# First slab on centred tokens: gate and up products scaled by ScalarE on the way out, its normalized tokens turned by one DMA, and the first y tiles seeded

## The chip, the cores and the metric

The kernel runs on one core of one Trainium2 chip. The metric is the device time of that core in microseconds (us), the median of repeated runs. One execution is recorded by the hardware profiler; all times inside the kernel below are counted from the start of that recorded span.

The core has a matrix engine (TensorE, "PE" in the profile), a vector engine (VectorE, "DVE"), an engine for functions of one operand (ScalarE, "ACT"), a general engine (GpSimd, "POOL"), and a queue engine (SyncE, "SP") that here issues nearly all DMA transfers. Each engine works through its own list of instructions in order and waits for semaphores of the others. "PEld" is the loading of a matmul's stationary operand, which runs beside PE.

## What is computed

For 2048 tokens `x` of width 512:

```python
xn = layernorm(x)                          # (x - mean) / sqrt(var + 1e-5), per token
# branch A: a complex diagonal recurrence of 512 states over time
Lam_bar = exp(dt * (Lambda_re + 1j * Lambda_im));  dt = exp(log_dt)
B_bar   = ((Lam_bar - 1) / Lam)[:, None] * (B_re + 1j * B_im)
Bu = einsum("bld,pd->blp", xn, B_bar)
h[t] = Lam_bar * h[t-1] + Bu[t]
s = 2 * einsum("blp,dp->bld", h, C_re + 1j * C_im).real + xn * Dskip
# branch B: a gated feed-forward layer of inner width 1376, then silu
g = silu((gelu(xn @ w_gate) * (xn @ w_up)) @ w_down)
out = x + s * g
```

The matrices and tokens are bf16.

## The kernel before

The tokens are worked in four slabs of 512 (`NS = 4`, `TS = 512`), a slab in four tiles of 128 tokens (`M = 4`). A tile's m below is 0 to 3. Tokens lie on the partitions when they are normalized, but a matmul needs the feature dimension there, so every normalized tile has to be turned (transposed): into `xnT`. Slab 0's tiles are turned by TensorE itself (a matmul with the identity into a spare PSUM bank, then a copy out of PSUM); the tiles of the later slabs are turned by a DMA (`dma_start_transpose`).

The instruction order on each engine isn't written down. The code collects steps with costs, and a planner in the kernel (`Plan`) sorts them by list scheduling and a random search; the text below therefore speaks of the order as built. TensorE's steps keep the order of the code.

Slab 0's gate and up products run in three chunks of columns, `CH0 = [(0, 384), (384, 896), (896, 1376)]`, each as pairs (gate in one PSUM bank, up in another) in one of three two-bank slots, one pair in the two spare banks `ybank`:

```python
def norm_dve(s, m):                      # VectorE, one pass: (x - mean) * rstd
    dve(512, lambda: V.tensor_scalar(out=xn[m][:], in0=x_tok[:, s * M + m, :],
        scalar1=mv[:, s, m, 0:1], scalar2=rs[:, s, m : m + 1],
        op0=ALU.subtract, op1=ALU.mult), ...)

def head_t(m):                           # turned by TensorE, copied out by ACT (m = 3: by DVE)
    transposed(xn[m], m, xnT[:, :, m * P : (m + 1) * P], [("xn", m)], [("xnT", 0, m)],
               m % 2, DVE if m == 3 else ACT)

def gate_pair(s, m, c, then=((), ()), spare=False):
    ...
    for bank, (nm, wt) in enumerate((("wg", wg), ("wu", wu))):
        def f(bank=bank, wt=wt):
            for k in range(KT):          # KT = 4
                T.matmul(pss[bank][:, 0:w], lhsT=xnT[:, k, t0 : t0 + P], rhs=wt[:, k, a:b], ...)
    acts(w, lambda: act(out=ud, in_=pss[1][:, 0:w], func=AF.Copy), both, [("ub", q)])
    acts(w, lambda: act(out=gd, in_=pss[0][:, 0:w], func=AF.Gelu_apprx_tanh), both, [("gt", q)], table="gelu", ...)
    dve(w, lambda: V.tensor_tensor(out=at[j][:, a:b], in0=gd, in1=ud, op=ALU.mult), ...)
```

`mv` holds mean and variance of a tile (from two VectorE instructions, L402 and L406), and `rs` its 1/sqrt(var + eps), a power computed by GpSimd (L409). The head of the program in the order of the code:

```python
dummies(6, 0); columns(); dummies(3, 0)           # dummy matmuls keep TensorE busy
stats(0, 0); mean(0, 0); rstd(0, 0, 1)
stats(0, 1); mean(0, 1); norm_dve(0, 0); rstd(0, 1, 2)
head_t(0); dummies(2, 0, 3); turn_angles(); angle(0)
norm_dve(0, 1); stats(0, 2); mean(0, 2); rstd(0, 2, 3); ...
stats(0, 3); norm_dve(0, 2); mean(0, 3); rstd(0, 3, 4); ...; norm_dve(0, 3)
tables()                                          # sine tables, on ACT and DVE
then = {0: ((lambda: head_t(1), spread), ()), 1: ((lambda: head_t(2),), ()), 2: ((lambda: head_t(3),), ())}
for m in range(M):
    gate_pair(0, m, 0, then.get(m, ((), ())), m == M - 1)
...
for m in range(M): gate_pair(0, m, 1)
for h in range(2): half(0, h)                     # B_bar products of slab 0, then the recurrence
for m in range(M): gate_pair(0, m, 2); at_t(0, m, 0, 2)
```

`half(s, h)` multiplies `BT` (the turned B matrices) with a slab's `xnT` on TensorE (L612), rotates the result by the tables, runs the scans and rotates back on VectorE, and leaves the states in `hst`. `at_t` turns the gated activations of a tile by DMA into `atT` (L527). `down_pair` multiplies `atT` with `wd` (L544), two tiles in one slot. Once slab 0's products are issued, slab 1 follows: `norm1` computes statistics and normalizes on VectorE, `dma_t` turns each tile (L453), `half(1, 0)` and `half(1, 1)` follow on TensorE, then `down_pair(0, 0)` (tiles 0 and 1) and `down_pair(0, 1)` (tiles 2 and 3). `norm_act(s)` does the normalization of slabs 2 and 3, with ScalarE for the sums and the scaling.

`y_tile` gives the output of branch A for a tile: eight matmuls of 512 columns (L574) into `ybank`, to which the skip term `sk = xn * Dskip` is added. From the third tile on ScalarE writes `sk` into the bank first ("seed") and the matmuls add to it; the first two tiles have no seed:

```python
if seed:
    acts(w, lambda: act(out=bank, in_=sk[s % 2][:, m, a:z], func=AF.Copy), ...)
...
if seed:
    dve(w, lambda: V.tensor_tensor(out=yg[e][:, a:z], in0=bank, in1=g2[gi][:, b, a:z], op=ALU.mult), ...)
else:
    dve(512, lambda: V.tensor_tensor(out=ys, in0=bank, in1=sk[s % 2][:, m, :], op=ALU.add), ...)
    dve(512, lambda: V.tensor_tensor(out=yg[e][:], in0=ys, in1=g2[gi][:, b, :], op=ALU.mult), ...)
```

All large transfers are issued by SyncE on one queue. As built, before: the four tiles of x of slab 0 mixed with the first weight chunks, second weight chunks, x of slab 1, `BT` (two DMA transposes of 512x512), third weight chunks, `wd`, four DMA transposes for slab 1's `xnT`, the two of C (into the memory of `hst[1]`), x of slabs 2 and 3, then the four `atT` of slab 0 in the order m = 0, 1, 3, 2.

Of the kernel before, what the change touches and what calls it, by code (L numbers as in the profile page):

```python
# [202 lines left out]
def kernel(  # L203
# [17 lines left out]
    nc = tc.nc  # L221
# [32 lines left out]
    xnT = sb("xnT", [P, KT, 2 * TS])  # L254
# [20 lines left out]
    xn = [sb(f"xn{i}", [P, D]) for i in range(M)]  # L275
# [5 lines left out]
    tF = sb("tF", [P, 2, D], FP32)  # L281
    junk = sb("junk", [P, D])
# [31 lines left out]
    def dma_first(eng, issue, land, emit, writes, **kw):  # L314

        first[eng] = dma(eng, issue, land, emit, writes=writes, after=[first[eng]] if eng in first else (), **kw)
# [29 lines left out]
    dma_first(SP, 1.45, 4.0, lambda: nc.sync.dma_start(out=x_tok[:, M : 2 * M, :], in_=x_r[:, M : 2 * M, :]), [("x", 1, m) for m in range(M)])  # L346
    for ri, src in enumerate((A_B_re, A_B_im)):
        dma_first(SP, 2.4, 4.0, lambda ri=ri, src=src: nc.sync.dma_start_transpose(out=BT[:, ri, :, :], in_=src), [("BT", ri)])
    for which in range(2):
        load_w(dma_first, SP, nc.sync, 2, (1.35, 4.1), which)  # L350
# [21 lines left out]
    def columns():  # L372

        pe(1, 150, lambda: T.matmul(rows, lhsT=pv[0][:], rhs=ident[0 : 2 * NPT, 0 : 2 * NPT], start=True, stop=True),
            [("pv", 0), ("pv", 1), "ident"], [("slot", 2, 0)])
        acts(4, lambda: act(out=dt_, in_=rows[:, 0:NPT], func=AF.Exp), [("slot", 2, 0), "tiny"], ["dt"], table="exp", rank=150.0)
        acts(1, lambda: act(out=tiny[:], in_=zero[:], func=AF.Sin), ["zero", "dt"], ["tiny"], table="silu", rank=150.0)
# [44 lines left out]
    def transposed(src, n, dst, reads, writes, bank, evict):  # L422
        tp = ybank[bank][:].bitcast(BF16)[:, 0:D].rearrange("p (k t) -> p k t", t=P)

        def f():
            for k in range(KT):
                T.transpose(tp[:, k, :], src[:, k * P : (k + 1) * P], ident[:])  # L427
        pe(KT, P, f, reads + ["ident"], [("y", bank)])
        if evict == ACT:
            acts(512, lambda: act(out=dst, in_=tp, func=AF.Copy), [("y", bank)], writes, rank=100.0)  # L430
        else:
            dve(512, lambda: V.tensor_copy(out=dst, in_=tp), [("y", bank)], writes, rate=2.0, rank=40.0)
# [10 lines left out]
    def norm_dve(s, m):  # L443
        dve(512, lambda: V.tensor_scalar(  # L444
            out=xn[m][:], in0=x_tok[:, s * M + m, :], scalar1=mv[:, s, m, 0:1], scalar2=rs[:, s, m : m + 1],
            op0=ALU.subtract, op1=ALU.mult), [("x", s, m), ("mv", s, m), ("rs", s, m)], [("xn", m)], rate=2.0)

# [3 lines left out]
    def dma_t(s, m):  # L451
        c0 = (s % 2) * TS + m * P
        return dma(SP, 1.2, 4.5 if s == 1 else 1.3, lambda: nc.sync.dma_start_transpose(out=xnT[:, :, c0 : c0 + P], in_=xn[m][:]),  # L453
            [("xn", m)], turned_tile(s, m))

    def skip(s, m):
        dve(512, lambda: V.tensor_tensor(out=sk[s % 2][:, m, :], in0=xn[m][:], in1=Drow[:], op=ALU.mult),
            [("xn", m), "Drow"], [("sk", s % 2, m)], rate=2.0)
# [4 lines left out]
    def gate_pair(s, m, c, then=((), ()), spare=False):  # L463

        if spare:
            pss, both = [ybank[0][:], ybank[1][:]], [("y", 0), ("y", 1)]
        else:
            i, ps = slot()
            pss, both = [ps[:, 0, :], ps[:, 1, :]], [("slot", i, 0), ("slot", i, 1)]
        a, b = CH0[c]  # L470
        w = b - a
        j = (s * M + m) % NAT
        t0 = (s % 2) * TS + m * P
        q = gu_n[0] % (2 * NGT)
        gu_n[0] += 1
        qb, qo = q // 2, (q % 2) * 512
        for bank, (nm, wt) in enumerate((("wg", wg), ("wu", wu))):
            def f(bank=bank, wt=wt):
                for k in range(KT):
                    T.matmul(pss[bank][:, 0:w], lhsT=xnT[:, k, t0 : t0 + P], rhs=wt[:, k, a:b], start=(k == 0), stop=(k == KT - 1))  # L480
            pe(KT, w, f, turned_tile(s, m) + [(nm, c)], [both[bank]])
            for t in then[bank]:
                t()
        gd, ud = gt[qb][:, qo : qo + w], ub[qb][:, qo : qo + w]
        acts(w, lambda: act(out=ud, in_=pss[1][:, 0:w], func=AF.Copy), both, [("ub", q)])
        acts(w, lambda: act(out=gd, in_=pss[0][:, 0:w], func=AF.Gelu_apprx_tanh), both, [("gt", q)], table="gelu", after=early if c == 0 else (), rank=40.0 if c + m == 0 else 0.0)
        dve(w, lambda: V.tensor_tensor(out=at[j][:, a:b], in0=gd, in1=ud, op=ALU.mult), [("gt", q), ("ub", q)], [("at", j, c)], rate=2.0)

    def gate_tile(s, m):

        j = (s * M + m) % NAT
        t0 = (s % 2) * TS + m * P
# [3 lines left out]
        def mm(ps, bank, wt, c):  # L496
            a, b = CH[c]

            def f():
                for k in range(KT):  # L500
                    T.matmul(ps[:, bank, 0 : b - a], lhsT=xnT[:, k, t0 : t0 + P], rhs=wt[:, k, a:b], start=(k == 0), stop=(k == KT - 1))  # L501
            return f
# [50 lines left out]
    def y_tile(s, m):  # L553
        i = y_n[0] % 2
        seed = y_n[0] >= 2
# [7 lines left out]
        for bank, key, a, z in parts:  # L563
            y_part(s, m, bank, key, a, z, i, e, gi, b, seed)

    def y_part(s, m, bank, key, a, z, i, e, gi, b, seed):

        w = z - a
        if seed:
            acts(w, lambda: act(out=bank, in_=sk[s % 2][:, m, a:z], func=AF.Copy), [("sk", s % 2, m)], [key])  # L570

        def f():
            for j in range(2 * NPT):
                T.matmul(bank, lhsT=hst[s % 2][:, j // NPT, j % NPT, m * P : (m + 1) * P], rhs=C2[:, j // NPT, j % NPT, a:z],  # L574
                         start=(j == 0 and not seed), stop=(j == 2 * NPT - 1), skip_group_check=True)
        pe(2 * NPT, w, f, [("hst", s % 2, 0), ("hst", s % 2, 1)] + C2S + ([key] if seed else []), [key])
        if seed:
            dve(w, lambda: V.tensor_tensor(out=yg[e][:, a:z], in0=bank, in1=g2[gi][:, b, a:z], op=ALU.mult),  # L578
                [key, ("g2", gi)], [("yg", e, a)], base=0.13)
        else:  # L580
            ys = tF[:, i, :]
            dve(512, lambda: V.tensor_tensor(out=ys, in0=bank, in1=sk[s % 2][:, m, :], op=ALU.add),
                [key, ("sk", s % 2, m)], [("tF",)], base=0.13)
            dve(512, lambda: V.tensor_tensor(out=yg[e][:], in0=ys, in1=g2[gi][:, b, :], op=ALU.mult),
                [("tF",), ("g2", gi)], [("yg", e, a)], base=0.13)
# [16 lines left out]
    def half(s, h):  # L602
# [3 lines left out]
        for q in range(H2):  # L606
            i, ps = slot()
            pt = h * H2 + q
            for ri in range(2):
                def f(ri=ri, pt=pt, ps=ps):  # L610
                    for k in range(KT):
                        T.matmul(ps[:, ri, :], lhsT=BT[:, ri, k, pt * P : (pt + 1) * P], rhs=xnT[:, k, (s % 2) * TS : (s % 2 + 1) * TS],  # L612
# [99 lines left out]
    def head_t(m):  # L712
        transposed(xn[m], m, xnT[:, :, m * P : (m + 1) * P], [("xn", m)], [("xnT", 0, m)], m % 2, DVE if m == 3 else ACT)

    def spread():
        pe(1, 512, lambda: T.matmul(slots[2][:, 1, :], lhsT=warm[0:1, 0:P], rhs=Drow[0:1, :], start=True, stop=True), ["Drow", "warm"], [("slot", 2, 1)])
        acts(512, lambda: act(out=Drow[:], in_=slots[2][:, 1, :], func=AF.Copy), [("slot", 2, 0), ("slot", 2, 1)], ["Drow"])
# [3 lines left out]
    dummies(3, 0)  # L721
# [3 lines left out]
    rstd(0, 0, 1)  # L725
    stats(0, 1)
    mean(0, 1)
    norm_dve(0, 0)
    rstd(0, 1, 2)
    head_t(0)  # L730
    dummies(2, 0, 3)
    turn_angles()
    angle(0)
    norm_dve(0, 1)
    stats(0, 2)
    mean(0, 2)
    rstd(0, 2, 3)
    angle(1)
    stats(0, 3)
    norm_dve(0, 2)  # L740
    mean(0, 3)
    rstd(0, 3, 4)
    angle(2)
    angle(3)
    norm_dve(0, 3)
    pl.in_turn = False
    tables()
    then = {0: ((lambda: head_t(1), spread), ()), 1: ((lambda: head_t(2),), ()), 2: ((lambda: head_t(3),), ())}
    for m in range(M):
        gate_pair(0, m, 0, then.get(m, ((), ())), m == M - 1)  # L750
        if m == 1:
            damping()
    dma_first(SP, 3.6, 4.3, lambda: nc.sync.dma_start(out=wd[:, 0 : NFT - 1, :], in_=B_w_down[0 : (NFT - 1) * P, :].rearrange("(k p) d -> p k d", p=P)), ["wd"])
    dma_first(SP, 0.4, 4.3, lambda: nc.sync.dma_start(out=wd[:FL, NFT - 1, :], in_=B_w_down[(NFT - 1) * P : F, :]), ["wd"])
    for m in range(M):
        skip(0, m)
    for m in range(M):
        gate_pair(0, m, 1)
    for h in range(2):
        half(0, h)  # L760
    for m in range(M):
        gate_pair(0, m, 2)
# [40 lines left out]
    def norm_out(s, m):  # L803
        acts(512, lambda: act(out=xn[m][:], in_=x_tok[:, s * M + m, :], func=AF.Identity, scale=rs[:, s, m : m + 1], bias=nb[:, s, m : m + 1]),
# [35 lines left out]
    for ri, src in enumerate((A_C_re, A_C_im)):  # L840
        dma(SP, 2.4, 5.0, lambda ri=ri, src=src: nc.sync.dma_start_transpose(out=CT[:, ri, :, :], in_=src),
            writes=[("CT", ri)], after=[turned[1]])
# [68 lines left out]
```

## Time and profile before

| what | value |
|---|---|
| time, median of 3 runs | 181.27 us (180.87 to 182.46) |
| recorded span | 179.6 us, granted TensorE clock 0.998 |
| TensorE busy | 173.4 us (97%) |
| VectorE busy | 157.8 us (88%) |
| ScalarE busy | 116.7 us (65%) |
| DMA queue of SyncE | 17.86 MB, 46.3% of 16 engines' span |
| first product of slab 0 on TensorE | at 6.21 us |
| second chunk's first product | at 13.41 us |
| first down product | at 40.61 us |

Read the busy shares first, then where the busiest engine is idle, and only then what the other engines do in those places. In the strip of 40 slices a slice is 4.49 us, and a digit is the busy share in tenths. Times in a timeline are the start of a merged run of instructions from its first to its last. A line such as "SPq" is the issue of a transfer, not the transfer: how long the data took is told apart, as the time from issue to landing.

### The profile page before, as it was taken

Reading aid. Unit: us, or ns where it says so; the run is one execution under the profiler, and the core shown is the slowest. Engines: PE = TensorE matmul, PEld = TensorE weight load, DVE = VectorE, ACT = ScalarE, POOL = GpSimd, SP = SyncE. Lnnn points to the kernel's source line nnn. Section 1 sums busy time; section 2 is a strip of 40 time slices with the busy share of each in tenths; the row PEclk is TensorE's granted clock in tenths of the full one; section 3 lists DMA queues with packets and bytes.
Section 4 is the critical chain, followed back from the end, with each engine's and each line's share of the span. In section 5 each row is a group of like instructions: output and inputs, shape, how many; then the busy total and the mean of one; then the engine's idle time right before and its main releaser. Section 6 shows DMA issues by size and latency. Waiting matters only on the chain.

```text
span 179.6 us, 2392 instructions
## 1 busy us (share of the span) xinstructions
PE 173.4 (97%) x838; PEld 82.6 (46%) x854; DVE 157.8 (88%) x268; ACT 116.7 (65%) x178; POOL 9.7 (5%) x19
## 2 busy tenths in 40 slices
PE   7999999999999999999999999999999999999992
PEld 2354444444445555444445554544445555444451
DVE  4789999998999999999999999999999999950063
ACT  4788599589999999645359964426618666353220
POOL 3230230000002000000020000000000000000000
PEclk9999999999999999999999999999999999999999
DMA  4999999997000429630011485050100084420011
GB/s 127 332 285 218 367 202 179 305 156 155 0 0 0 80 57 114 130 61 0 0 60 62 93 155 109 1 111 4 58 29 0 2 160 84 82 86 29 0 58 58
DMA packets 47109, 18.01 MB, mean 100 GB/s; under 512 B 38425, under 2 KB 47098, under 8 KB 47098
## 3 DMA queue, kind: packets, MB, share of 16 engines
q1 hardware_dynamic: 47072, 17.86, 46.3%
q8 instruction: 6, 0.10, 0.2%
q14 instruction: 5, 0.04, 0.1%
q10 hardware_dynamic: 26, 0.00, 0.0%
HBM read 6.33 MB, written 2.10 MB: 47 GB/s over the span
## 4 chain that ended last, share of the span: by engine, by line
PE 90%; DMA 4%; DVE 2%; SPq 1%; issue 1%; DVEq 0%
PE slot L501 31%; PE slot L544 21%; PE slot L612 15%; PE ybank L574 13%; PE slot L480 9%; DMA x_tok<-in_A_x_dram 3%; DMA out_dram<-ot 1%; DVE ot L586 1%; PE ybank L480 1%; SPq L328 1%; DVE yg L578 1%; SPq L321 1%; DVE st L402 0%; PE ybank L427 0%; DVE xn L444 0%
## 5 line engine op out<-in xcount | busy, mean ns | idle before, releaser
L501 PEld LDWEIGHTS <-xnT 128*128 128x128 bf16 x288 | 28.2, 98 | 28.4
L544 PE MATMUL slot<-wd,atT 128*128 128x512 bf16 (+1 forms) x173 | 38.5, 379 | 0.2
L501 PE MATMUL slot<-wu,xnT 128*128 128x512 bf16 (+1 forms) x144 | 31.8, 357 | 0.0
L501 PE MATMUL slot<-wg,xnT 128*128 128x512 bf16 (+1 forms) x139 | 31.5, 356 | 0.3
L645 DVE TENSOR_TENSOR_SCAN Fs<-rho,ini,W 128x512 bf16<-128x512 f32 x24 | 29.4, 1269 | 0.0
L612 PE MATMUL slot<-xnT,BT 128*128 128x512 bf16 x124 | 28.1, 379 | 0.2
L574 PE MATMUL ybank<-C,hst 128*128 128x512 bf16 (+1 forms) x125 | 27.6, 372 | 0.2
L544 PEld LDWEIGHTS <-atT 128*128 128x128 bf16 (+1 forms) x176 | 17.2, 98 | 20.9
L615 ACT ACTIVATE U<-slot 128x1024 bf16<-128x1024 f32 x16 | 16.0, 1021 | 12.5 <-PE slot L612 12.5
L578 DVE TENSOR_TENSOR yg<-ybank,g 128x512 bf16<-128x512 f32 (+1 forms) x14 | 9.4, 670 | 12.8 <-PE ybank L574 12.5
L574 PEld LDWEIGHTS <-hst 128*128 128x128 bf16 x136 | 13.3, 98 | 13.8
L612 PEld LDWEIGHTS <-BT 128*128 128x128 bf16 x128 | 12.5, 98 | 15.1
L626 DVE TENSOR_TENSOR Q<-U,tab 128x4096 bf16<-128x4096 bf16 x8 | 18.3, 2289 | 0.2
L626 DVE TENSOR_TENSOR Q<-Fs,tab 128x4096 bf16<-128x4096 bf16 x8 | 18.3, 2289 | 0.1
L548 ACT ACTIVATE g<-slot 128x1024 f32<-128x1024 f32 x8 | 8.2, 1021 | 13.4 <-PE slot L544 13.4
L570 ACT ACTIVATE ybank<-sk 128x512 f32<-128x512 bf16 (+1 forms) x14 | 8.1, 586 | 12.7 <-DVE yg L578 12.0
L509 ACT ACTIVATE gt<-slot 128x1024 bf16<-128x1024 f32 x12 | 12.3, 1023 | 3.7 <-PE slot L501 3.7
L509 ACT ACTIVATE ub<-slot 128x1024 bf16<-128x1024 f32 x12 | 12.2, 1020 | 3.0 <-PE slot L501 2.8
L480 PEld LDWEIGHTS <-xnT 128*128 128x128 bf16 x96 | 9.0, 98 | 9.7 <-ACT xnT L430 0.7
L823 ACT ACTIVATE junk<-x_tok 128x512 bf16<-128x512 bf16 x16 | 10.0, 627 | 1.6 <-DMA x_tok<-in_A_x_dram 1.4
L480 PE MATMUL slot<-wg,xnT 128*128 128x480 bf16 (+2 forms) x43 | 10.4, 360 | 0.4 <-ACT xnT L430 0.4
L480 PE MATMUL slot<-wu,xnT 128*128 128x512 bf16 (+2 forms) x44 | 10.4, 360 | 0.0
(118 smaller groups left out, 179.1 us busy)
## 6 DMA issues: line engine op xcount, KB each, us to landing
out_dram<-ot SPq DMA_DIRECT2D x15, 128.0 KB, 1.7
x_tok<-in_A_x_dram SPq DMA_DIRECT2D x3, 512.0 KB, 5.8
wd<-in_B_w_down_dram SPq DMA_DIRECT2D x1, 1280.0 KB, 9.9
x_tok<-in_A_x_dram SPq DMA_DIRECT2D x4, 128.0 KB, 3.0
wg<-in_B_w_gate_dram SPq DMA_DIRECT2D x1, 512.0 KB
wu<-in_B_w_up_dram SPq DMA_DIRECT2D x1, 512.0 KB, 6.9
wg<-in_B_w_gate_dram SPq DMA_DIRECT2D x1, 480.0 KB, 5.0
wu<-in_B_w_up_dram SPq DMA_DIRECT2D x1, 480.0 KB
```

Source lines behind the costliest of these rows:

```text
L480: T.matmul(pss[bank][:, 0:w], lhsT=xnT[:, k, t0 : t0 + P], rhs=wt[:, k, a:b], start=(k == 0), stop=(k == KT - 1))
L501: T.matmul(ps[:, bank, 0 : b - a], lhsT=xnT[:, k, t0 : t0 + P], rhs=wt[:, k, a:b], start=(k == 0), stop=(k == KT - 1))
L509: acts(1024, lambda ps=ps, dst=dst, fn=fn: act(out=dst[:, 0:1024].rearrange("p (c w) -> p c w", c=2), in_=ps[:, :, :], func=fn), [("slot", ...
L544: T.matmul(ps[:, b, :], lhsT=atT[:fs, k, m * P : (m + 1) * P], rhs=wd[:fs, k, :], start=(k == 0), stop=(k == NFT - 1))
L548: acts(1024, lambda: act(out=g2[gi][:, :, :], in_=ps[:, :, :], func=AF.Silu), [("slot", i, 0), ("slot", i, 1)], [("g2", gi)], table="silu" ...
L574: T.matmul(bank, lhsT=hst[s % 2][:, j // NPT, j % NPT, m * P : (m + 1) * P], rhs=C2[:, j // NPT, j % NPT, a:z], start=(j == 0 and not seed ...
L578: dve(w, lambda: V.tensor_tensor(out=yg[e][:, a:z], in0=bank, in1=g2[gi][:, b, a:z], op=ALU.mult), [key, ("g2", gi)], [("yg", e, a)], base ...
L612: T.matmul(ps[:, ri, :], lhsT=BT[:, ri, k, pt * P : (pt + 1) * P], rhs=xnT[:, k, (s % 2) * TS : (s % 2 + 1) * TS], start=(k == 0), stop=(k ...
L615: acts(1024, lambda q=q, ps=ps: act(out=U[ui][:, :, q, :], in_=ps[:, :, :], func=AF.Copy), [("slot", i, 0), ("slot", i, 1)], [("U", ui, q)])
L626: dve(4096, lambda: V.tensor_tensor(out=Qf, in0=src.unsqueeze(1).to_broadcast(WQ), in1=table, op=ALU.mult), reads, ["Q"], rate=2.0)
L645: pl.add(DVE, 1.116 if s == 0 else 1.19, lambda ri=ri, q=q, pt=pt, first=first: V.tensor_tensor_scan(out=Fs[:, ri, q, :], data0=rho[:, pt ...
L823: acts(512, lambda i=i, fn=fn, m=m: act(out=junk[:], in_=x_tok[:, s * M + m, :], func=fn, accum_out=sx[:, s, i, m : m + 1]), [("x", s, m)] ...
```

## The change

Three things are altered in slab 0 and in the first y tiles, and with them the order of the transfers.

1. For the first two chunks (c = 0 and 1) the gate and up products no longer take normalized tokens but tokens less their mean. A row's 1/sqrt(var + eps) is one number per token, so it can be applied to the row of the product: ScalarE applies it as it copies the product out of PSUM (`scale=rs[...]`, one number per partition, for the copy of up and before the gelu of gate alike). The turning by TensorE then waits for the mean alone and not for GpSimd's power.
2. The normalized tokens of slab 0 are still needed: for the B products, for chunk 2 and for the skip term. They are computed later, and turned all four tiles at once by one DMA.
3. The first two y tiles are seeded as the others are.

The centred tokens use memory that is free then (`Fs`, and `W` for the turned ones). The transfers are re-ordered: x of slab 1 is no longer loaded ahead of `BT`, C comes ahead of slab 1's turning, and `wd` behind it. The diff, cut to its core:

```diff
-    xnT = sb("xnT", [P, KT, 2 * TS])
+    xnT = [sb(f"xnT{i}", [P, KT, TS]) for i in range(2)]
+    xc = [Fs[:, i // 2, i % 2, :] for i in range(M)]
+    xcT = W[:].rearrange("p r q t -> p (r q t)").rearrange("p (m k t) -> p m k t", m=M, k=KT)
...
-    dma_first(SP, 1.45, 4.0, lambda: nc.sync.dma_start(out=x_tok[:, M : 2 * M, :], ...)
-    for ri, src in enumerate((A_B_re, A_B_im)):  ... BT ...
-    for which in range(2):
-        load_w(dma_first, SP, nc.sync, 2, (1.35, 4.1), which)
+    def load_rest():
+        ... BT, re and im ...
+        dma_first(SP, 2.0, 3.5, lambda: nc.sync.dma_start_transpose(
+            out=xnT[0]... , in_=xn_all[:].rearrange("p m d -> p (m d)")), ...)
+        ... x of slab 1, third chunk of wg and wu, C re and im ...
...
+    def center(m):
+        dve(512, lambda: V.tensor_scalar(out=xc[m], in0=x_tok[:, m, :], scalar1=mv[:, 0, m, 0:1],
+            scalar2=None, op0=ALU.subtract), [("x", 0, m), ("mv", 0, m)], [("xc", m)], rate=2.0)
...
+            kw, rd, ptr = {}, [], 0
+            if self.bare:                      # chunks 0 and 1
+                kw, rd, ptr = dict(scale=rs[:, 0, m : m + 1]), [("rs", 0, m)], 1
+            acts(w, lambda: act(out=ud, in_=pss[1][:, 0:w], func=AF.Copy, **kw), ...)
+            acts(w, lambda: act(out=gd, in_=pss[0][:, 0:w], func=AF.Gelu_apprx_tanh, **kw), ...)
...
-    dummies(3, 0)
+    dummies(1, 0)
     stats(0, 0); mean(0, 0)
-    rstd(0, 0, 1)
+    center(0)
     stats(0, 1); mean(0, 1)
-    norm_dve(0, 0); rstd(0, 1, 2); head_t(0); dummies(2, 0, 3)
+    center(1); rstd(0, 0, 2)
     ...
+    head_t(0, ACT); dummies(2, 0); behind = [head_t(1, ACT)]
+    ... # sine table of ACT asked for only now
+    pairs = [GatePair(m, 0, m == M - 1) for m in range(M)]
+    pairs[0].products(0); spread(); pairs[1].products(0); pairs[0].products(1)
+    head_t(2, ACT); pairs[1].products(1); damping(); pairs[2].products(0)
+    head_t(3, DVE); norm_dve(0, 1); norm_dve(0, 2); norm_dve(0, 3)
+    pairs[2].products(1); pairs[3].products(0); pairs[3].products(1)
...
     norm1()
-    for ri, src in enumerate((A_C_re, A_C_im)): ... C ...
+    first[SP] = turned[1]
+    ... wd, in two transfers ...
```

In `y_part` the branch without a seed is removed. The last pair of chunk 1 goes to the spare banks, so that the slots of the pairs behind it move by one; the sequence of products on TensorE is otherwise as before from chunk 0's end on.

## The prediction

> **What bounds the kernel now.** I read the busy shares first, then the waits of TensorE, then the chain of waits, then the timeline of the first 50 us.
>
> ```profile
> PE 173.4 (97%) x838; PEld 82.6 (46%) x854; DVE 157.8 (88%) x268; ACT 116.7 (65%) x178; POOL 9.7 (5%) x19
> ...
> DMA  4999999997000429630011485050100084420011
> ```
>
> TensorE is busy 97% of the span. The DMA strip has nines until about 45 us: the transfers are full exactly where the change re-orders them. The waits of TensorE up to 60 us:
>
> ```profile
> PE slot L419 <- DVE zero L362: 1.1, 1, 1.1
> PE ybank L427 <- DVE xn L444: 0.4, 1, 0.4
> PE slot L480 <- ACT xnT L430: 0.4, 1, 0.4
> ```
>
> All three lie before 10 us; from 14 us to the end the same view is empty. From the chain of waits (start, duration, what):
>
> ```profile
> 3.23 5.05 DMA x_tok<-in_A_x_dram
> ...
> 8.30 0.69 DVE st L402
> ...
> 9.36 0.40 PE ybank L427 x4
> ...
> 12.23 1.34 PE ybank L480 x8
> 13.58 0.21 PE slot L480
> 13.84 6.64 PE slot L480 x30
> ```
>
> x of tile 3 lands at 8.28, and VectorE finishes its statistics ahead of normalizing tile 2, so tile 2 is turned only at 9.36. Behind that TensorE runs without a hole. So a gain can come only from starting the second chunk earlier than 13.41, and every new hole behind it is lost in full.
>
> The tight places further on are transfers. From the timeline:
>
> ```profile
> 16.17 2.26 SPq L754 DMA_DIRECT2D wd<-in_B_w_down_dram  x1
> 19.88 5.92 SPq L453 DMA_TRANSPOSE xnT<-xn  x4
> 25.85 2.02 SPq L841 DMA_TRANSPOSE hst<-in_A_C_re_dram  x1
> 27.93 2.59 SPq L841 DMA_TRANSPOSE hst<-in_A_C_im_dram  x1
> 30.56 1.13 SPq L819 DMA_DIRECT2D x_tok<-in_A_x_dram  x2
> 31.79 10.07 SPq L527 DMA_TRANSPOSE atT<-at  x4
> 40.61 7.73 PE L544 MATMUL slot<-wd,atT 128*128 128x512 bf16 x34
> ```
>
> The first atT transfer is issued at 31.79 and lands 8.0 us later, at 39.8 (DMA view of that window): 0.8 before the down products that read it. The other three, issued at 36.15, 38.49 and 40.44, take 3.8 at most, so the last (m = 2) is there at about 44; it is needed two tiles, 22 x 0.216 = 4.75 us, after 40.61, at 45.4. Slack 1.4.
>
> **What the Trainium skill says.** "ScalarE: Activation LUTs", section What ACT_TABLE_LOAD costs: each per-partition pointer operand adds about 93 ns to an ACTIVATE. The trace agrees in kind: 1024 elements with a scale pointer (L844) take 1.15 us, without one (L615) 1.02. I use the trace's 0.13. The same section gives 1283 ns for a table load; here it is 1.28. "DMA: Bandwidth & Descriptors", section Queues, rings and completion order: descriptors of a queue are consumed in ring order on each DMA engine. The landings here follow the issues in that order, so what is put ahead in the queue delays what stands behind. "TensorE: Matmul & The Clock Gate", Part 1: about 3.4 us of activity warm the clock up. Here a 512-column dummy takes 2.74/6 = 0.46 us at first, and 384 columns 0.16 from 7.5 us on. The change keeps TensorE similarly busy from 1.05, so I expect the same warm-up.
>
> **The change at the start.** I replay the built order of the changed kernel with durations of this trace.
>
> VectorE: statistics of tile 0 at 2.85, mean 3.58, centring 3.80 to 4.18. Tile 1 centred at 5.44. Tile 2's x is there at 5.95, so statistics 6.2, centred 7.53. Then the angle operations, to 8.45; statistics of tile 3 at 8.45 (landed 8.28), mean 9.15, centred 9.75. Before, the four normalized tiles were ready at 5.06, 6.21, 9.31 and 10.91.
>
> TensorE: tile 0 turned at 4.3, tile 1 behind two dummies at 5.6, first product at about 5.85 (the weights landed 3.9 us after their issue at 1.66). Gate 0, the Dskip spread, gate 1, up 0: 3 x 0.65 + 0.21, to 8.0. Tile 2 turned, 8.2; up 1 to 8.9. Gate 2 waits for ScalarE, which has copied tile 1 by 6.5, then loads a table (1.28), does the tiny activation and the Drow copy, and copies tile 2 from 8.5 to 9.1. So gate 2 from 9.2 to 9.85; tile 3 turned by 10.3, copied by VectorE to 10.7; up 2 meanwhile; gate 3 and up 3 from 10.8 to 12.1. The first chunk ends at 12.1 and not at 13.41: 1.3 us.
>
> But the second chunk needs slot 0 free, that is its gelu done. ScalarE behind 9.0: two sine operations (0.73), scaled up copy (0.42 + 0.13), two small copies (0.45), table load 1.28, gelu 0.49 + 0.13: ends at 12.65. **TensorE starts chunk 1 at 12.7; gain 0.7 us.** The 16 scaled activations add 16 x 0.13 = 2.1 us to ScalarE, but by its slots the replay finds no other hole for TensorE before the B products: chunk 1 ends at 19.6.
>
> **The single turning DMA.** BT lands about 1.5 earlier than before without the x of slab 1 ahead of it (14.8 and 16.9 become 13.3 and 15.4). All 512 tokens are as many 256-byte packets as one BT half, 2.1 us: xnT lands at about 17.5. Needed at 19.6, so hidden.
>
> **What is pushed back.** x of slab 1 lands at 19.7 and not at 12.6; VectorE has its statistics behind three table operations, from 20.2 to 22.9, then four gating products and a table operation of 1.14, and normalizes from 24.85 to 26.4 where it was 19.45 to 21.2. The four turning DMAs, 1.2 us of issue each, go from 25.3 to 30.1 and land by 31.6; they are needed at 33.0. Hidden, with 1.4 to spare.
>
> wd stands behind them: issued at 30.15, its 1.4 MB take 4.5 us (as between the landings of the third up chunk at 21.1 and of wd at 25.5), so it lands at 36.2. Needed at 39.9. Then atT m = 0 (1408 packets, 1.8 us): 38; x of slabs 2 and 3 (3.0): 41; atT m = 1, 3, 2 (1.6 each): 42.6, 44.2, 45.8. Before, x and the first atT together took 6.7 us from the landing of C at 33.1 to 39.8, and not the 4.8 of this sum: mixed copies and transposes run slower. With up to 1.9 for that, m = 2 lands between 46 and 48. TensorE wants it at 45.4 - 0.7 = 44.7. **A new wait of 1.1 to 3 us before the last two tiles' down products; I take 1.7.**
>
> **Seeds of the first y tiles.** Two additions of 0.69 us leave VectorE, two ScalarE copies of 0.59 come in at about 21, and TensorE's work is equal. No direct effect. But in the built order slab 2's variance now stands behind the first y tile's gate product, while before it was done at 56 us, 10 ahead of it. From the end of y tile 0 on TensorE: gate product 0.6, four small operations 0.6, power and bias with the W addition beside it 1.5, ScalarE's first tile 0.9, three issues of 1.3, landing 2.6: 10.1 us. TensorE has 9.7 us of other work before it wants slab 2's xnT (65.96 to 75.65). **Another wait of about 0.4.**
>
> Sum: 181.27 - 0.7 + 1.7 + 0.4 = 182.7. I say 182.5, since slower transfers are the least certain term and the sum has no room for a gain there.
>
> **Rivals.** First: the transfers keep up, as the change means them to, and the start is all that counts. For it: VectorE may be done with slab 1 earlier than I replay, and every earlier us of the turning moves wd by as much. Against it: the 0.8 and 1.4 of slack shown above. The time would then be about 180.6. Second: the single turning lands late, because a transpose out of SBUF is slower than one out of DRAM (packets of mixed stretches are slower here as said). Then the B products wait at 19.6 instead; 2 us late would make 183 to 184. Third: VectorE becomes the bound. It is 88% busy and starts the first recurrence at 27.5 where it was 26.6; the last C operation of slab 0 ended at 62.4 before and y begins at 64.2. With 0.9 later and y 0.7 earlier this still fits, and any wait for transfers gives it more room, so no more than a few tenths.
>
> **Range and chances.** Gain at the start 0.3 to 1.1; waits 0 to 4. That spans 180.4 to 184.8. 2% is 3.6 us: a gain of that size isn't there, since TensorE's holes before 13.4 don't hold it. A loss of it needs two of the waits at their worst.
>
> **What would show it.** In the changed profile: first product near 5.85, second chunk near 12.7 and 0.05 behind a gelu; no wait at the first B products near 19.6; wd issued near 30; a wait of TensorE for atT within the down products of 40 to 48 us, of 1 to 3 us; a smaller one before slab 2's B products near 75. The prediction is wrong if TensorE's waits behind 14 us are empty again, if it waits for the single turning, or if the start gains over 1.3.

## The result, and the profile after

| | median | runs | ratio to before, 95% interval |
|---|---|---|---|
| before | 181.02 us | 6 runs, 180.87 to 182.46 | |
| after | 185.98 us | 6 runs, 185.30 to 187.03 | 1.0267 [1.0217, 1.0316] |

The change makes the kernel slower by 2.7%, and the time lies 1.2 us above the predicted range. The page of the kernel after, its busy shares, granted clock and DMA strip (a slice is 4.61 us):

```profile
PE 175.8 (95%) x852; PEld 82.6 (45%) x852; DVE 158.5 (86%) x268; ACT 119.9 (65%) x180; POOL 8.8 (5%) x17
...
PEclk9999999999799999999999999999999999999999
DMA  5999994999200167550001355440300074060012
```

VectorE's busy time is as before (158.5 against 157.8), and TensorE's share fell from 97% to 95%. The 7 in the clock row, at 46 to 51 us, is the first sign of something else. The waits of TensorE (total us, times, longest us):

```profile
PE slot L572 <- DMA atT<-at: 2.2, 1, 2.2
PE slot L432 <- DVE zero L376: 1.1, 1, 1.1
PE ybank L600 <- ACT ybank L596: 0.8, 1, 0.8
PE ybank L440 <- DVE Fs L461: 0.3, 1, 0.3
PE slot L631 <- DMA xnT<-xn: 0.2, 1, 0.2
PE slot L500 <- ACT gt L513: 0.2, 1, 0.2
```

Before, this list was empty from 14 us on. Now three of its rows lie behind 40 us. TensorE's timeline shows where (start, duration, instruction, count, idle time just before and what ended it):

```profile
12.42 1.02 PE L500 MATMUL slot<-wg,W 128*128 128x512 bf16 x4 [0.22 <-ACT gt L513]
...
39.90 2.55 PE L572 MATMUL slot<-wd,atT 128*128 128x512 bf16 x11
44.65 8.99 PE L572 MATMUL slot<-wd,atT 128*128 128x512 bf16 x33 [2.20 <-DMA atT<-at]
53.48 1.89 PE L529 MATMUL slot<-wg,xnT 128*128 128x512 bf16 x8
...
78.26 1.89 PE L600 MATMUL ybank<-C,hst 128*128 128x512 bf16 x8 [0.85 <-ACT ybank L596]
80.39 1.89 PE L631 MATMUL slot<-xnT,BT 128*128 128x512 bf16 x8 [0.25 <-DMA xnT<-xn]
```

Read it by its starts. The second chunk begins at 12.42, 0.99 earlier than before. The 11 down products of tile 0 end near 42.3 (39.90 + 11 x 0.216), and those of tile 1 start at 44.65. The 33 products from there to 53.48 take 8.83 us, where 33 x 0.216 is 7.1. The same starts of both kernels give the account:

| TensorE starts | before | after | after less before | new in this stretch |
|---|---|---|---|---|
| second chunk | 13.41 | 12.42 | -0.99 | -0.99 |
| first down product | 40.61 | 39.90 | -0.71 | +0.28, atT of m = 0 |
| slab 1's gate products | 50.13 | 53.48 | +3.35 | +4.06, atT of m = 1 and slow products |
| first y tile | 64.07 | 67.42 | +3.35 | 0 |
| slab 2's B products | 75.62 | 80.39 | +4.77 | +1.42, seed and slab 2's xnT |

From there to the end the two run alike: the spans are 179.6 and 184.3. The 4.06 split into 44.65 - 42.28 = 2.37 of wait and 1.7 of slow products. The same count gives the 1.42: 78.26 - 73.79 - 16 x 0.216 = 1.02 at the seed and 80.39 - 78.26 - 8 x 0.216 = 0.40 at xnT. The windows view of the stretch around the slow products (window, length, busy us and count of PE, PEld, DVE, ACT and POOL, granted clock, DMA share, GB/s):

```profile
39.80:44.65 4.85, 2.55 (x11) 1.00 (x12) 4.85 (x14) 3.72 (x5) 0.00 (x0) 1.00 1.18 286
44.65:53.50 8.85, 8.85 (x34) 3.67 (x35) 6.85 (x12) 3.74 (x7) 0.00 (x0) 0.81 0.31 62
45.22:48.63 3.41, 3.41 (x10) 1.21 (x8) 3.38 (x8) 0.00 (x0) 0.00 (x0) 0.50 0.57 108
48.63:53.50 4.87, 4.87 (x24) 2.16 (x23) 2.90 (x4) 3.39 (x6) 0.00 (x0) 1.00 0.01 3
```

From the end of the wait to 53.5 the granted clock is 0.81 on average, and 7.13 / 0.81 = 8.8 us is the duration seen. In detail it is 0.50 for 3.41 us, from 45.22 to 48.63, and 1.0 around that: half of 3.41 is the 1.7 lost. Not every execution has this dip: three of the six have a mean clock of 0.991 and spans of 184.3 to 185.2, the other three 1.0 and 183.5 to 184.1. The profile shows one of the first kind.

### The profile page after: what moved, and what is told of

The parts are those of the page before. It is cut to its first block, busy times and chain, and to the rows that moved or that the text cites. A ratio compares the mean times of both kernels' runs of the same rounds, so it can differ in the third digit from the quotient of the medians.

```text
span 184.3 us, 2408 instructions
## 1 busy us (share of the span) xinstructions
PE 175.8 (95%) x852; PEld 82.6 (45%) x852; DVE 158.5 (86%) x268; ACT 119.9 (65%) x180; POOL 8.8 (5%) x17
## 4 chain that ended last, share of the span: by engine, by line
PE 65%; DVE 16%; DMA 9%; ACT 5%; issue 2%; POOL 1%; SPq 0%; DVEq 0%
PE slot L529 27%; PE slot L572 20%; PE ybank L600 9%; PE slot L631 8%; DVE Fs L664 4%; DMA atT<-at 4%; DMA x_tok<-in_A_x_dram 4%; DVE st L415 2%; DVE Q L645 2%; DVE at L515 1%; DMA xnT<-xn 1%; DVE Q L712 1%; POOL rs L422 1%; ACT junk L864 1%; DMA out_dram<-ot 1%
## 5 line engine op out<-in xcount | busy, mean ns | idle before, releaser
L572 PE MATMUL slot<-wd,atT 128*128 128x512 bf16 (+1 forms) x176 | 40.6, 391 | 2.3 <-DMA atT<-at 2.2
L529 PEld LDWEIGHTS <-xnT 128*128 128x128 bf16 x288 | 28.2, 98 | 28.4
L529 PE MATMUL slot<-wu,xnT 128*128 128x512 bf16 (+1 forms) x144 | 31.8, 357 | 0.0
L529 PE MATMUL slot<-wg,xnT 128*128 128x512 bf16 (+1 forms) x144 | 31.8, 357 | 0.0
L600 PE MATMUL ybank<-C,hst 128*128 128x512 bf16 (+1 forms) x128 | 28.1, 372 | 0.8 <-ACT ybank L596 0.8
L572 PEld LDWEIGHTS <-atT 128*128 128x128 bf16 (+1 forms) x176 | 17.4, 100 | 24.9 <-DMA atT<-at 3.3
L603 DVE TENSOR_TENSOR yg<-ybank,g 128x512 bf16<-128x512 f32 (+1 forms) x16 | 10.6, 670 | 12.5 <-PE ybank L600 12.0
L600 PEld LDWEIGHTS <-hst 128*128 128x128 bf16 x136 | 13.3, 98 | 14.8 <-issue 1.1
L645 DVE TENSOR_TENSOR Q<-U,tab 128x4096 bf16<-128x4096 bf16 x8 | 18.3, 2287 | 0.3
L645 DVE TENSOR_TENSOR Q<-Fs,tab 128x4096 bf16<-128x4096 bf16 x8 | 18.3, 2288 | 0.2
L596 ACT ACTIVATE ybank<-sk 128x512 f32<-128x512 bf16 (+1 forms) x16 | 9.3, 587 | 11.5 <-DVE yg L603 11.5
L664 DVE TENSOR_TENSOR_SCAN Fs<-rho,W 128x512 bf16<-128x512 f32 x8 | 9.4, 1209 | 0.0
L500 PEld LDWEIGHTS <-W 128*128 128x128 bf16 x64 | 5.9, 98 | 5.9 <-issue 0.4
L547 DVE TENSOR_TENSOR at<-gt,ub 128x1024 bf16<-128x1024 bf16 x12 | 8.2, 680 | 0.0
```

The source lines that it names most:

```text
L529: T.matmul(ps[:, bank, 0 : b - a], lhsT=xnT[s % 2][:, k, t0 : t0 + P], rhs=wt[:, k, a:b], start=(k == 0), stop=(k == KT - 1))
L547: dve(1024, lambda: V.tensor_tensor(out=at[j][:, 0:1024], in0=gt[q][:, 0:1024], in1=ub[q][:, 0:1024], op=ALU.mult), qs[0] + qs[1], [("at", ...
L572: T.matmul(ps[:, b, :], lhsT=atT[:fs, k, m * P : (m + 1) * P], rhs=wd[:fs, k, :], start=(k == 0), stop=(k == NFT - 1))
L645: dve(4096, lambda: V.tensor_tensor(out=Qf, in0=src.unsqueeze(1).to_broadcast(WQ), in1=table, op=ALU.mult), reads, ["Q"], rate=2.0)
L664: pl.add(DVE, 1.116 if s == 0 else 1.19, lambda ri=ri, q=q, pt=pt, first=first: V.tensor_tensor_scan(out=Fs[:, ri, q, :], data0=rho[:, pt ...
```

## The experiments

In all of them but e8 the order of every instruction is frozen as built in the changed kernel, and only the steps named are moved. The line numbers are six higher there (L572 is L578, L529 is L535, L600 is L606). The runs of the kernel before beside them had medians of 181.00 to 181.11.

### e1 and e10: x of slabs 2 and 3 behind the atT transfers

```diff
 SyncE: ..., slab 1's turning, wd, atT m = 0,
-  x of slabs 2 and 3, atT m = 1, m = 3, m = 2
+  atT m = 1, m = 3, m = 2, x of slabs 2 and 3
```

> The changed kernel with its order of instructions frozen; only the loads of x of slabs 2 and 3 are put behind the four atT transfers of slab 0 (and ScalarE's first sum over slab 2 ahead of the second, where it was 5 us earlier). Theory (queue order): TensorE's wait of 2.2 us for the second atT comes from 3 us of x put ahead of it. The second atT then lands at about 41.5 and not 44.6, needed at 42.3; the wait goes, and with it the stretch of slower matmuls behind it (1.65 us). Expected 182.0 us (181.4 to 182.8), that is 4 us below the changed kernel's 186.0; the later wait before slab 2 stays. Rival (the engines are late, not the queue): the activations or the weights of the down product hold the second tile back; then the time stays within 0.5 of 186.0.

Measured: 182.94 us, ratio 1.0087 [1.0058, 1.0115]. This one move takes back 3.0 of the 5.0 us. The one execution with a profile ran at a mean clock of 0.562 and took 310.63 us, so the same kernel ran again:

> The same kernel as the first experiment (x of slabs 2 and 3 behind the four atT transfers), for a profile of an undisturbed execution. Theory: about 182.9 as there; no wait for atT but 0.3 at m = 0; B products of slab 2 start with a wait for xnT of 1.5 to 2.5 us, since the sums and the power of slab 2 now stand behind x that lands at 47 or later.

Measured: 182.56 us (181.82 to 182.98), ratio 1.0078 [1.0055, 1.0100]. Its profile is that of its fastest execution. TensorE's timeline and its waits:

```profile
39.72 9.68 PE L578 MATMUL slot<-wd,atT 128*128 128x512 bf16 x44
49.23 1.89 PE L535 MATMUL slot<-wg,xnT 128*128 128x512 bf16 x8
```

```profile
PE ybank L606 <- ACT ybank L602: 0.9, 1, 0.9
PE slot L637 <- DMA xnT<-xn: 0.2, 1, 0.2
```

All 44 down products run in one piece; the second tile's atT landed at 41.2 and not at 44.6. The clock has no dip near the down products: with the wait, the slow products are gone too. No execution of e1 or e10 but the one of 310.63 us had a mean clock under 0.998. My guess for the xnT wait (1.5 to 2.5) missed: what is left there are the 0.85 and 0.25 of the kernel after, 1.1 in all. So the x transfers were **not** what delayed slab 2.

### e2: wd ahead of slab 1's turning

```diff
 SyncE: ...,
-  C, slab 1's turning, wd, atT m = 0, x of slabs 2 and 3, ...
+  wd, slab 1's turning, C, atT m = 0, x of slabs 2 and 3, ...
```

> The changed kernel frozen; only the order of the queue is altered: wd goes ahead of slab 1's turning and C behind it, as before the change; x of slabs 2 and 3 still stand ahead of the second atT. The bytes ahead of the second atT are the same, but the queue has wd's data to move while the turning waits for VectorE (in the changed kernel's trace nearly idle from 28.0 to 32.2 between the landing of C and of the last turned tile). Theory (a gap in the queue): the second atT lands about 2 us earlier, near 42.5, the wait shrinks to 0.3 or less and the slower stretch goes: 182.3 us (181.5 to 183.5). Rival (bytes alone count): no change, 186.0.

Measured: 184.57 us, ratio 1.0196 [1.0173, 1.0219], between the two and above the range. The queue does have a gap in the kernel after. Its DMA view of 28 to 40 us, in slices of 0.3 us:

```profile
DMA  0892049600991047968999999878999996999979
```

The zeros are the pauses between slab 1's turning DMAs, which are issued 1.3 us apart and each keep the engines busy for a part of that. Behind them wd starts its stream only at some 32.3. With wd ahead, atT m = 0 lands at 38.27 and not at 39.85. But x then takes from there to 42.65, 4.4 us where it took 3.6, and m = 1 lands at 43.94, only 0.66 earlier. TensorE's timeline:

```profile
43.98 2.55 PE L578 MATMUL slot<-wd,atT 128*128 128x512 bf16 x11 [1.68 <-DMA atT<-at]
47.13 4.93 PE L578 MATMUL slot<-wd,atT 128*128 128x512 bf16 x22 [0.60 <-DMA atT<-at]
```

Here the clock stays up, and the second wait, for m = 2, is seen that the slow products cover in the kernel after. What is ahead of m = 1 in the queue decides, more than when the queue starts.

### e3: TensorE kept busy through the wait

```diff
 TensorE: down products of tile 0
+  10 matmuls of 512 columns into a free slot, results unused
 TensorE: down products of tile 1
```

> The changed kernel frozen; ten idle matmuls of 512 columns on data already there (their result is overwritten unused) are put between the down products of tile 0 and tile 1, where TensorE waits 2.2 us for a transfer; they take 10 x 0.216 = 2.2 us, as long as the wait. Theory (the wait makes TensorE's clock fall, and the 33 products behind it take 8.8 us and not 7.1): the granted clock stays at 1.0 and the time falls by 1.6, to 184.3 (183.8 to 184.9). Rival (the slow stretch has another cause, such as transfers into the operands, or comes by chance): the added work changes nothing or costs up to 0.5 us, 186.0 to 186.5.

Measured: 187.16 us, ratio 1.0333 [1.0293, 1.0372]; both expectations missed. In the profiled execution the clock is 1.0, but the timeline has a longer wait for m = 2:

```profile
44.86 2.55 PE L578 MATMUL slot<-wd,atT 128*128 128x512 bf16 x11
49.18 4.93 PE L578 MATMUL slot<-wd,atT 128*128 128x512 bf16 x22 [1.77 <-DMA atT<-at]
```

m = 2 landed at 49.13 instead of 47.73. In the DMA view of that window one packet of 16 KB of another queue, kind "instruction", stands among the 256-byte packets of the transpose:

```profile
q1 hardware_dynamic: 3120, 0.77, 91.9%
q8 instruction: 1, 0.02, 1.2%
```

In the trace it stands at 46.31, with the transpose still moving; in the kernel after the same packet comes at 48.65, when the last transpose has landed. My reading is that the extra matmuls shifted the fetch of the program into this transfer; that this delayed it is argued, not shown. Nor is the clock settled by this run: one of its four executions had a mean of 0.994 and a span of 186.1, against 184.4 to 184.8. What the experiment does show is that the slow products are not a loss in full: where the clock stays up, the products wait for m = 2 instead, here 1.77 us, and 0.6 in e2 and e4.

### e4: slab 2's normalization ahead of the first y tile

```diff
 ScalarE:
-  sums of slab 2 spread up to the first y tile; the four xn of slab 2 behind it
+  sums of slab 2 in one piece, from the landing of x on; the four xn between the gelus of slab 1
 VectorE, GpSimd:
-  variance and power of slab 2 behind the first yg product
+  variance and power of slab 2 17 us earlier (power at 53.9, not 70.7)
```

> The changed kernel frozen; slab 2's normalization is taken out from behind the first y tile: ScalarE's seven sums go into its idle time ahead of the first silu (near 44 us), variance and power follow near 52, ScalarE scales the four tiles between the gelus of slab 1's third tile, and their turning goes ahead of the third atT of slab 1. Theory: between the first y tile and slab 2's B products the changed kernel loses 80.39 - 67.42 = 12.97 against 75.62 - 64.07 = 11.55 us before, all of it in this chain; the 1.4 us come back: 184.6 (184.0 to 185.3). Rival (the seeds hold TensorE up: the wait of 0.85 for ScalarE's copy is what counts, and the turning isn't late by itself): the gain is at most 0.6.

Measured: 184.48 us (183.86 to 185.78), ratio 1.0208 [1.0156, 1.0260], 1.5 below the kernel after. TensorE's waits behind 40 us:

```profile
PE slot L578 <- DMA atT<-at: 2.9, 2, 2.3
```

Neither the seed nor xnT is waited for: slab 2's B products follow the y tiles at once. The four executions also tell the worth of the dip. Two with a mean clock of 0.988 to 0.989 have spans of 183.2 and 184.0, two at 1.0 have 182.1 and 182.2: some 1.0 to 1.9 us, in half of the executions. The profiled one is without the dip, although its first wait for atT, 2.34 us, is longer than the 2.20 of the kernel after.

### e8: the seeds alone, in the kernel before

```diff
-  y tiles 0 and 1: VectorE adds sk to the finished product, then multiplies
+  y tiles 0 and 1: ScalarE writes sk into the bank at 21 us, the products add to it, VectorE multiplies
```

> The kernel before with the third part of the change alone: the first two y tiles seeded by ScalarE copies in place of VectorE's two additions, the order of all other instructions kept as before. Theory of the prediction (no direct effect): 181.0 within 0.2. Rival (VectorE's 1.4 us less work before the last y tiles, or the ScalarE copies ahead of a gelu, show): 180.3 or 181.6.

The order of the kernel before is kept. In this run the output lacks part of the skip term of those two tiles; the instructions and their counts are those of the seed. My reading of the lack rests on the Trainium skill, "PSUM — Partial Sum Buffer", section PSUM: the matmul accumulator: an accumulation's first matmul clears the written marks of the whole bank, and a later one adds only where a mark is set. The last products in those banks had marked only 384 of 512 columns; no run here separates it. Measured: 181.08 us against 181.08, ratio 0.9991 [0.9973, 1.0009]. The third part has no effect by itself.

### e5, e6 and e7: the repairs together

```diff
 e5 = e4 and:
   SyncE: ..., wd, atT m = 0,
-    x of slabs 2 and 3, atT m = 1, m = 3, m = 2
+    atT m = 1, x of slab 2, atT m = 2, m = 3, x of slab 3
 e6 = e5 and e2's order of wd, the turning and C
 e7 = e6 and ScalarE's copies of the angle tables behind the gelu of tile 0
```

> The changed kernel with slab 2's statistics, power and normalized tiles moved ahead of the first y tile (as in the run before) and with the transfers in the order atT m = 0, m = 1, x of slab 2, m = 2, m = 3, x of slab 3. Theory (all of the loss is the wait for atT behind the two x transfers, the clock dip beside it, and the late chain of slab 2; the gain of 1.0 at the start is sound): about 180.3, so 0.5 to 1.0 us below the kernel before; only about 0.3 us of wait at atT m = 0 is left, and no wait behind it. Rival (the shared queue is simply fuller, and whatever stands behind waits): 182 or more, with the wait moved to m = 2 or to x of slab 2.

> As the run above, and wd issued ahead of slab 1's turning, C behind it, so that the queue has no gap before wd. Theory: atT m = 0 lands at about 38.3 and its 0.3 us of wait goes too: 180.0. Rival (C behind the turning comes late for VectorE's state products and pushes y back): 180.5 to 181.5, with waits of TensorE near the first y tile.

> As the run above, and ScalarE's small copies of the angle tables moved behind the gelu of tile 0, so that slot 0 comes free earlier. Theory: the second chunk starts 0.2 to 0.35 us earlier than at 12.42, and all behind it follows: 179.7. Rival (the angle tables are what VectorE waits for, so the copies moved back are paid later): no gain over the run above, VectorE idle near 13 us.

| | median, range | ratio, 95% interval | expected |
|---|---|---|---|
| e5 | 184.31 (183.36 to 185.17) | 1.0167 [1.0136, 1.0197] | 180.3 |
| e6 | 183.49 (182.97 to 184.04) | 1.0131 [1.0110, 1.0151] | 180.0 |
| e7 | 183.26 (182.88 to 183.64) | 1.0118 [1.0100, 1.0137] | 179.7 |

All three missed by 3.5 to 4 us. The step that e7 adds is worth less than expected too: the second chunk starts at 12.35 where e6 has 12.51. In e6 no wait for a transfer is left, and yet TensorE waits, for ScalarE:

```profile
PE slot L535 <- ACT gt L543: 1.0, 1, 1.0
PE ybank L606 <- ACT ybank L602: 0.9, 1, 0.9
```

The second of them leads to VectorE. Its timeline in e6:

```profile
46.67 2.34 DVE L670 TENSOR_TENSOR_SCAN Fs<-rho,W 128x512 bf16<-128x512 f32 x2
52.06 0.75 DVE L893 SCALAR_TENSOR_TENSOR C<-hst,cre,tF 128x512 bf16<-128x512 bf16 x1 [3.06 <-ACT tF L891]
```

and ScalarE's, with the instruction that VectorE waits for:

```profile
47.94 0.63 ACT L870 ACTIVATE junk<-x_tok 128x512 bf16<-128x512 bf16 x1
48.48 0.19 ACT L870 ACTIVATION_READ_ACCUMULATOR junk<-x_tok 128x1 f32 x1
48.68 1.28 ACT L582 ACT_TABLE_LOAD   x1
49.97 1.02 ACT L582 ACTIVATE g<-slot 128x1024 f32<-128x1024 f32 x1
50.89 1.14 ACT L891 ACTIVATE tF<-hst,cim 128x1024 f32<-128x1024 bf16 x1
```

My edit had put eight sums of slab 2 in a row; the product tF stood behind them, and VectorE idled for 3.06 us. Its product of y tile 1, which frees the bank of the last seed, then came at 74.23, where e9 has it at 72.00: that is the 0.9 at the seed. The 1.0 at gt needs no VectorE: ScalarE works without a pause from 41.5 to 55.3, and its gelus stand behind the same row of sums. In e4 VectorE had the same hole, 3.22 us, and TensorE no such waits: as I read it, because there TensorE itself stood still for 2.9 us. This was a fault of the repair, not of the change.

### e9: the same, with the sums spread again

```diff
 ScalarE, from 42 us on:
-  8 sums, g (with table), tF, g, gelu and up of slab 1, ...
+  3 sums, tF, 1 sum, g (with table), 2 sums, g, gelu and up of slab 1, tF, ..., 1 sum, ..., 1 sum, ...
```

> As the last of the three runs before it (queue without a gap, x of slabs 2 and 3 between the atT transfers, slab 2 early, angle copies behind the first gelu), but with ScalarE's eight sums of slab 2 spread between its other work as in the kernel before, and the two tF products back at their places ahead of the gelus. Theory (those three runs paid back their gain because eight sums in a row held up ScalarE's tF, so that VectorE stood idle for 3.06 us from 49.0 and the y tiles and their seeds came late): no wait of TensorE at gt and at the ybank seed any more, 1.9 us and the 0.7 lost behind it come back: 180.0, from 179.7 to 180.4. Rival (VectorE has too little room in the first slab without the x of slab 1 and the third part of the change): 181.5 or more, with VectorE without a hole from 27 to 75 us and TensorE waiting for C or hst near the y tiles.

Measured: 180.38 us (180.32 to 180.93), ratio to before 0.9960 [0.9947, 0.9974], in the range expected. This is faster than both kernels by little: the change with these repairs gains 0.7 us. Whether one of the repairs, such as the later copies of the angle tables, would gain in the kernel before was not run. All of TensorE's waits behind the first 5 us:

```profile
PE slot L535 <- ACT gt L543: 0.5, 1, 0.5
```

And its timeline, at the places of the account above:

```profile
12.13 1.03 PE L506 MATMUL slot<-wg,W 128*128 128x512 bf16 x4
...
39.60 9.69 PE L578 MATMUL slot<-wd,atT 128*128 128x512 bf16 x44
...
75.25 7.07 PE L637 MATMUL slot<-xnT,BT 128*128 128x512 bf16 x32
```

The second chunk starts 1.28 earlier than before and the down products 1.01 earlier; 0.48 is then paid at gt, where ScalarE is late with sums that could start only when x of slab 2 had landed at 42.9, and at slab 2's B products 0.37 is left in this execution (span 179.2; the other four had 178.5 to 178.7). VectorE has one hole of 0.18 us between 24 and 82 us, and TensorE waits for it nowhere.

## Why the prediction was wrong, point by point

- **Start, -0.7.** Right in kind, 0.3 too small: the second chunk started at 12.42, as predicted 0.05 behind a gelu that frees slot 0 and not behind its operands. The 0.13 for a scale pointer came from two lines that read different memories. The same copies of 384 columns, 0.49 to 0.50 before, take 0.58 with the pointer: 0.09, close to the 93 ns that the prediction quoted and set aside. By the first down product 0.7 was left, since atT m = 0, put at 38, landed at 39.85. e9 shows that the gain survives to the end where transfers and ScalarE let it. No run separates the centred tokens from the other changes at the head, such as fewer dummy matmuls.
- **The single turning DMA and slab 1's turning, hidden.** Right: landed at 18.3 (predicted 17.5, needed 19.3) and at 32.2 (31.6, needed 32.7). The rival of a late single turning did not happen.
- **The wait for atT, +1.7.** This step failed: the wait was 3.0, and it began a tile earlier than I looked for it. I had listed m = 1 as landing at 42.6, up to 1.9 later with mixed transfers, but looked for the wait only before the last two tiles. Tile 1 is needed 11 products behind the first, at 39.9 + 2.4 = 42.3, ahead of even the early figure. The landings came at the late end of what I had worked out: m = 1 at 44.60, m = 2 at 47.73, where 45.8 + 1.9 = 47.7 stood. The lateness was not where I had put it, in x mixed with atT: wd, put at 36.2, landed at 38.44 (its last part is issued at 31.64 and takes 6.8), and from there m = 1 took 6.16 us where I had 6.4. Without a clock dip the waits add up to 2.4 + 0.6 = 3.0 (2.9 in e4), the upper end of the 1.1 to 3; I chose 1.7. What can be moved is the x of slabs 2 and 3 ahead of m = 1: with it behind, the wait goes (e1, e10), while wd ahead alone brings m = 1 only 0.66 forward (e2).
- **The clock: no term in the sum.** It is new, up to 1.7 us of slow products. About 1.1 of it is net, since 0.6 would be waited for m = 2. The prediction used the Trainium skill's "TensorE: Matmul & The Clock Gate", Part 1, only for the warm-up at the start. The same part says that the clock falls behind an idle window of about 3.4 us. Here it fell behind a wait of 2.2 us, and by the mean clocks it did so in half of the executions of the kernel after and of e4, so for a wait that comes near that figure the measurement has to decide. It is not what put the time above my range: the three executions without a dip took 185.3 to 185.86 us too.
- **Slab 2's chain, +0.4.** This step named the right chain and put it at less than a third of its size: it cost 1.42, 1.02 at a seed and 0.40 at xnT. The order that I had named, variance behind the first gate product, was as named, and moving it took the waits away (e4). The term mis-sized is GpSimd's power with the operations around it: 1.5 us assumed for power and bias, 2.29 from the power's start to the bias's end. The bias also holds up three scans and, behind them, the product that frees the bank of the last seed; that wait I hadn't listed. GpSimd and VectorE in the kernel after:

```profile
70.74 2.10 POOL L422 TENSOR_TENSOR rs<-sx,mhalf 128x4 f32<-128x4 f32 x1 [44.39 <-ACT ybank L596]
70.76 1.22 DVE L657 TENSOR_TENSOR W<-Q 128x2048 bf16<-128x2048 bf16 x1
...
72.87 0.16 DVE L875 SCALAR_TENSOR_TENSOR nb<-sx,rs 128x4 f32<-128x4 f32 x1 [0.90 <-POOL rs L422]
```

- **Seeds, no direct effect.** Right by e8. In the changed order the seed of the last y tile of slab 0 is waited for, because VectorE's yg product (76.99) stands behind the three scans; that wait goes with slab 2's chain in e4.
- **VectorE becomes the bound.** I gave it no more than a few tenths, and in the kernel after it is none: VectorE idles behind the waits. e6 shows how close the rival is: with VectorE's product 2.2 us later, TensorE waited 0.9 at a seed.

The sum, with its terms as measured in an execution with the dip: 181.0 - 1.0 + 0.3 (m = 0) + 3.0 (m = 1, m = 2) + 1.1 (clock, net) + 1.4 = 185.8, against 186.09 of that execution. Without the dip it is 184.7, and the other three took 185.3 to 185.86, so some 0.6 to 1.2 of them is unexplained. What stays open: e10's executions differ by 1.2 us (181.82 to 182.98) and only the fastest has a profile, so where the others lose the rest isn't known.

## What to carry to other kernels

When an early stage is sped up by moving loads behind it, write down for each transfer in the queue its landing **and its own first use**, tile by tile: the one that fails is the first that is late, not the last. Put what is used soonest first in the queue: x of slab 3 was first read near 68 us (e6), slab 2's variance had been taken at 56 before, and 1 MB of the two ahead of a 0.36 MB transfer needed at 42 cost 3 us. Operations moved together for convenience (eight sums in a row) hold up whatever stands behind them in an in-order engine, and VectorE, busy 86% to 88% of the span, has little room for it.

## What the runs showed of the hardware

- **TensorE's clock can fall behind a wait of 2.2 us, and need not.** Behind 2.20 us it was 0.50 for 3.41 us (kernel after); a wait of 2.34 left it at 1.0 (e4's profile), as did 1.68 (e2). So the length alone doesn't decide. The traces allow a reading: in the kernel after the recorded clock changes at 4.26, 45.22 and 48.63, which are 12 and 1 times 3.413 apart. If idling counts within such stretches, the wait from 42.45 to 44.65 lies whole in the one that ends at 45.22. In e4 the first change is at 5.71, so a stretch ends at 43.26, within the wait from 42.52 to 44.86, and splits it into 0.7 and 1.6. No run tests this.
- **GpSimd's power of 512 numbers took 1.0 to 2.1 us.** 2.10 beside an addition of 2048 bf16 elements (after, and again in e10), 1.78 beside scans of 1.17 (e6), 1.05 beside four products of 0.36 (e9). The Trainium skill's "GPSIMD Engine Reference", Specifications, says that GpSimd's SBUF interfaces are shared with VectorE and contended by its instructions with two SBUF inputs. The traces agree in part: in the kernel after the power ends 0.86 behind the end of that addition, but the four products have two such inputs too. No run isolates it.
- **The same 1 MB of x took 3.6 us or 4.4 us in the same queue.** From the landing of atT m = 0 to that of the second x it was 39.85 to 43.43 in the kernel after and 38.27 to 42.65 in e2, with other transfers ahead of it. What makes the difference isn't isolated.
